# Attention with routed experts: gate probabilities made per batch and stored with the rows, one VectorE operation per expert tile, slot 30's row stores on SyncE's queue

## The chip, the cores and the metric

The kernel runs on one core of one Trainium2 chip. The metric is the device time of one execution in microseconds; lower is better. The core has five engines with instruction queues of their own: TensorE (PE in the profile, with its weight loads as PEld), VectorE (DVE), ScalarE (ACT), GpSimd (POOL) and SyncE (SP). Each works through its queue in order. Transfers are issued from SP's queue and from POOL's queue and are carried out by the same 16 DMA engines.

## The reference

Eight batches, eight heads, 576 positions, 64 columns a head. Causal attention in blocks of 64; its output, put side by side over the heads, is the input x (4608 rows of 512) of a layer of eight experts.

```
scores = scale * (q @ k^T), masked by blocks of 64;  attn = softmax(scores);  x = attn @ v
logits = x @ w_gate                     # 8 per row
local_gate = sigmoid(x @ w_local)
for s in rows of a batch:
    e = argmax(logits[s]) if s == 0 or local_gate[s] < 0.5 else the expert of row s-1
    p = softmax(logits[s])
    out[s] = p[e] * (relu(x[s] @ w1[e]) @ w2[e])
```

So each row goes through one expert, and its result is scaled by the probability of that expert.

## The kernel before

**Attention.** One pair of heads is a slot; slot i holds pair i of 32, four slots a batch, some 7.5 us each. In a slot PE computes scores (L957), ACT their Exp (L967), PE the product with v (L978, L987), DVE adds the partial sums (L999, L1001), and PE turns k and q of the next pair by transposes (L668, kq). POOL brings the k and q of the pair after that into order (L860), from loads that SP issues (L847). Work of the batch before is laid into the slots: `half_batch` multiplies x by the gate weights on PE (L681, trg), `logits_of` makes the logits in the tile `L` (PE trl, DVE L770 to L779), and `rows_of_batch` turns x into rows: PE transposes (trx), DVE multiplies by the softmax factor (L799) and writes 512 bf16 numbers of a row tile, and POOL copies the 8 logits of each row into the tail behind them (L794, L798). A row tile of 128 rows, x and logits, goes to the array `x_rows` in HBM by `store` and `release` (L653). Stores are held back until the end of a slot and then released on POOL's queue; the last ones, from the end of slot 31 on, on SP's queue. Row tiles are made in tiles `xg` or, for the late ones, in two buffers `x`, which a new row tile can only take when the old one's store has landed.

**Routing.** The generators `tokens`, `slots_first` and `slots_second` find the expert of each row and put rows of one expert together in tiles of 128 (index tables idx0 and idx1, one for batches 0 to 4, one for the rest). Their steps are laid between other work by the class `Steps`, by weights in the code; the order on each engine is therefore fixed when the program is built. The last group runs beside the first expert tiles (`late`), together with the row tiles of the last batch (`rows`, `rows_out`), and DVE does most of it.

**Expert tiles.** 38 tiles are computed; 15 come from the first table. For a tile POOL gathers 128 rows with their tails (L626), SP transposes x (a DMA transpose, L1357; the first four are issued in slot 30, L1246, behind the loads of that slot), DVE copies the expert's first weight (L1329; L1057 for the first two tiles), PE makes the first product (L1072, `first_mm`), ACT applies Relu (L1075), PE makes the second product (L1275, `second_mm`), ACT scales by the factor (L1283) and POOL scatters the rows to the output (L1286). The factor is the probability of the chosen expert, made from the 8 logits in the tail: `exps_of` takes their maximum on DVE (L1340) and Exp with its sum on ACT (L1341), `factor_of` picks the expert's value (L1347), takes the reciprocal of the sum (L1349) and multiplies (L1350). The gathers of the second table wait until routing's last group and the last batch's rows are done (`gathers`).

The 1 MB weight loads (L107, L111) run from POOL's queue, one every other slot; the last, of w2 of expert 7, is issued in slot 30.

Of the kernel before, what the change touches and what calls it, by code (L numbers as in the profile page):

```python
# [62 lines left out]
def kernel(  # L63
# [11 lines left out]
    nc = tc.nc  # L75
# [121 lines left out]
    lim = rt_c.tile([P, E], F32, tag="lim", name="lim")  # L197
    less_e = rt_c.tile([P, E], F32, tag="less_e", name="less_e")
# [118 lines left out]
    def tokens(c0, c1, T, A):  # L317
# [5 lines left out]
        lg = L[:, cs, :E]  # L323
        mx = T([P, n], "mx")
        nc.vector.reduce_max(mx, lg, axis=AX)
# [316 lines left out]
    held = []  # L642
# [89 lines left out]

    def rows_out(b, t):
# [21 lines left out]
    def logits_of(b):  # L755
# [8 lines left out]
        def out():  # L764
# [14 lines left out]
            nc.vector.reduce_sum(Lb[:ST, 4], tmp[:ST, 0].rearrange("q h e -> q e h"), axis=AX)  # L779
        return out  # L780

    def rows_of_batch(b, ts):
# [6 lines left out]
        def out():  # L789
# [3 lines left out]
            if kept:  # L793
                nc.gpsimd.tensor_copy(xg[:n, t0:t1, XH:], L[:n, NC * b + t0:NC * b + t1, :E])  # L794
            for j, t in enumerate(ts):
                x = xs[j]
                if not kept:
                    nc.gpsimd.tensor_copy(x[:n, XH:], L[:n, NC * b + t, :E])  # L798
# [11 lines left out]
    with tc.tile_pool(name="atn_const", bufs=1) as cst, \  # L810
# [340 lines left out]
        def behind(i):  # L1151
# [24 lines left out]
        for i in range(NPAIR):  # L1176
# [61 lines left out]
            if i < NPAIR - 1:  # L1238
                release(queue=nc.gpsimd)
# [27 lines left out]
    with tc.tile_pool(name="ffn_s", bufs=2, reuse_waits="tile") as f_p, \  # L1267
# [26 lines left out]
        def late():  # L1294
# [6 lines left out]
            yield "V", 0.4  # L1301
# [36 lines left out]
        def exps_of(x, f):  # L1338

            nc.vector.reduce_max(f[:, 16:17], x[:, XH:], axis=AX, negate=True)  # L1340
            nc.scalar.activation(f[:, :8], x[:, XH:], func=AF.Exp, bias=f[:, 16:17], scale=1.0,  # L1341
                                 accum_out=f[:, 17:18])
            return f

        def factor_of(ph, j, f):

            nc.vector.scalar_tensor_tensor(f[:, 8:16], less_e, ids[ph][:, j:j + 1], f[:, :8],  # L1347
                                           op0=ALU.is_equal, op1=ALU.mult, accum_out=f[:, 18:19])
            nc.vector.reciprocal(f[:, 17:18], f[:, 17:18])  # L1349
            nc.vector.tensor_mul(f[:, 19:20], f[:, 18:19], f[:, 17:18])  # L1350
            return f[:, 19:20]
# [129 lines left out]
```

## Time and profile before

| | |
|---|---|
| time, three runs | 416.65, 416.87, 421.27 us; median 416.87 |
| the profiled execution's own time | 415.86 us |
| its span | 414.1 us |
| PE busy | 395.3 us (95%) |
| DVE busy | 257.2 us (62%) |
| ACT busy | 234.2 us (57%) |
| POOL busy | 194.4 us (47%) |

A matmul's end is modelled in the records, so PE's busy time tells where PE had nothing to do rather than how fast it worked. Attention takes the span to about 253 us, the expert tiles the rest. In the rows of the order of time the first number is the start, the second the time from the first to the last end of the merged instructions; in square brackets stands the idle time before and what ended it. SPq and POOLq are the engines' sequencers, where transfers are issued.

### The profile page before, as it was taken

To read this page: it belongs to the slowest core of one execution; us is meant where nothing else is said; L and a number is where in the kernel's file an instruction comes from. 1 tells how busy PE (TensorE), PEld (TensorE's weight loads), DVE (VectorE), ACT (ScalarE), POOL (GpSimd) and SP (SyncE) were. 2 spreads that over 40 slices of the span, in tenths; PEclk is the share of its full clock that TensorE was granted. 3 is DMA by queue.
4 is the path that set the end of the run, shared out by engine and by line. 5 is a ranking of instruction groups with operands and counts; after the bars stand their busy time and mean duration, and the time that the engine had idled before them with its cause. 6 is when DMAs were issued, how large, how long until landed. Compare 5 with 4: busy or idle time off the path is not lost. (4 is left out here: it accounts for less than half of the span.)

```text
span 414.1 us, 14752 instructions
## 1 busy us (share of the span) xinstructions
PE 395.3 (95%) x5827; PEld 285.7 (69%) x5827; DVE 257.2 (62%) x652; ACT 234.2 (57%) x463; POOL 194.4 (47%) x263
## 2 busy tenths in 40 slices
PE   8999999999999999999998996999999999999985
PEld 7677776876866876766876674666676677767653
DVE  3443847557577877679899563888894454444430
ACT  4666665764764765754764564343454565555543
POOL 1346256146145155136244340655658556777703
PEclk9999999999999999999999999899999999999989
DMA  6479998998998989997989789344535644654522
GB/s 184 118 175 242 208 195 231 211 189 211 220 183 212 212 161 251 202 203 193 212 171 263 145 171 159 102 126 111 156 113 146 142 122 137 150 151 129 131 71 77
DMA packets 106677, 70.25 MB, mean 170 GB/s; under 512 B 72703, under 2 KB 98111, under 8 KB 106608
## 3 DMA queue, kind: packets, MB, share of 16 engines
q0 software_dynamic: 18880, 35.08, 39.8%
q1 hardware_dynamic: 87728, 34.21, 33.6%
q8 instruction: 48, 0.79, 0.8%
q14 instruction: 21, 0.17, 0.1%
HBM read 67.02 MB, written 14.83 MB: 198 GB/s over the span
## 5 line engine op out<-in xcount | busy, mean ns | idle before, releaser
L999 DVE TENSOR_TENSOR S<-S,Pc 128x896 f32<-128x896 f32 (+2 forms) x96 | 87.0, 906 | 19.9 <-PE o L978 15.3
L957 PE MATMUL sc<-qkT 64*64 64x224 f32 (+6 forms) x1536 | 90.9, 364 | 0.0
L860 POOL COPY w_bf<-w_bf 128x512 f32<-128x512 f32 x61 | 52.0, 870 | 64.5 <-DMA w_bf<-in_k_dram 49.7
L1072 PEld LDWEIGHTS <-w1c 128*128 128x128 bf16 x1152 | 67.9, 98 | 14.4 <-issue 6.9
L1329 DVE COPY w1c<-w_bf 128x4096 bf16 x36 | 44.9, 1248 | 48.4 <-PE ps_y L1275 25.1
L1275 PE MATMUL ps_y<-w_bf,hT 128*128 x304 | 73.2, 384 | 0.3 <-issue 0.2
L1072 PE MATMUL ps_h<-xT,w1c 128*128 128x128 bf16 x1088 | 68.5, 220 | 4.8 <-ACTq L1441 2.0
L957 PEld LDWEIGHTS sc<-qkT 64*64 64x64 f32 x1536 | 70.2, 133 | 2.0 <-issue 0.5
L967 ACT ACTIVATE Pc<-sc 128x448 f32<-128x448 f32 (+1 forms) x96 | 68.3, 718 | 0.0
L1286 POOL DMA_INDIRECT out_dram<-y,idx x38 | 47.2, 1242 | 40.8 <-ACT y L1283 22.4
L626 POOL DMA_INDIRECT xg<-x_rows,idx x38 | 48.8, 1285 | 26.8 <-ACT hT L1075 11.6
L1075 ACT ACTIVATE hT<-ps_h 128x512 bf16<-128x512 f32 x76 | 42.8, 587 | 29.0 <-PE ps_y L1275 14.8
L978 PE MATMUL o<-Pc,v 128*64 128x320 f32 (+2 forms) x512 | 57.3, 366 | 0.0
L978 PEld LDWEIGHTS o<-Pc,v 128*64 128x64 f32 x512 | 34.7, 137 | 23.9
L1275 PEld LDWEIGHTS <-hT 128*128 128x128 bf16 x304 | 28.4, 99 | 29.4 <-issue 3.2
L967 ACT ACTIVATE S<-sc 128x576 f32<-128x576 f32 x64 | 42.0, 656 | 11.4 <-PE sc L957 11.4
L991 ACT COPY oT<-o 128x576 f32<-128x576 f32 x32 | 20.5, 641 | 34.7 <-PE o L987 34.3
L978 PE MATMUL o<-S,v 128*64 128x192 f32 (+1 forms) x256 | 34.7, 392 | 1.7 <-ACT qkT L905 1.7
L1283 ACT ACTIVATE y<-ps_y,f 128x512 f32<-128x512 f32 (+1 forms) x38 | 25.8, 680 | 12.8 <-PE ps_y L1275 9.3
L799 DVE TENSOR_TENSOR xg<-trx,rs 128x512 bf16<-128x512 f32 (+1 forms) x31 | 20.2, 684 | 20.5 <-PE trx L668 20.4
L690 ACT COPY LT<-trg 128x320 f32<-128x320 f32 x15 | 6.4, 425 | 44.2 <-PE trg L681 40.4
L926 ACT COPY qkT<-kq 128x1024 f32<-128x1024 f32 x30 | 30.9, 1031 | 0.3 <-PE kq L668 0.3
(268 smaller groups left out, 474.1 us busy)
## 6 DMA issues: line engine op xcount, KB each, us to landing
w_bf<-in_moe_w_dram POOLq DMA_DIRECT2D x16, 1024.0 KB
w_bf<-in_k_dram SPq DMA_DIRECT2D x32, 256.0 KB
w_bf<-in_q_dram SPq DMA_DIRECT2D x32, 256.0 KB
v<-in_v_dram SPq DMA_DIRECT2D x64, 128.0 KB
x_rows<-xg POOLq DMA_DIRECT2D x24, 132.0 KB
qkl<-in_k_dram SPq DMA_DIRECT2D x32, 32.0 KB
qkl<-in_q_dram SPq DMA_DIRECT2D x32, 32.0 KB
vl<-in_v_dram SPq DMA_DIRECT2D x32, 32.0 KB
```

Of the source, the lines that this page charges most:

```text
L626: st = nc.gpsimd.indirect_dma_start(out=x, out_offset=None, in_=x_dram[:rows], in_offset=bass.IndirectOffsetOnAxis(ap=row_of(ph, j), axis= ...
L860: copies[j](m, raws[i][1 + j].rearrange("p h j d -> p j h d"))
L926: nc.scalar.copy(to.rearrange("p a (r s) -> p r a s", r=2), ps.rearrange("p r (a s) -> p r a s", a=2))
L957: nc.tensor.matmul(to[:, col + skip:col + n], lhsT=t[r, 0, k0:k0 + ST], rhs=t[r, 1, q0 + skip:q0 + n], start=True, stop=True)
L967: nc.scalar.activation(exps_at(i, c, q0, n, rows), ps[rows, :, col:col + n], func=AF.Exp, scale=scale_attn)
L978: nc.tensor.matmul(po[64 * h:64 * h + 64, VO + q0:VO + q0 + n], lhsT=vs[i][c][:, h, :], rhs=exps_at(i, c, q0, n, slice(0, P))[:, h, :], st ...
L999: nc.vector.tensor_add(Ss[i][:, :, P * c:], Ss[i][:, :, P * c:], Pc[i % 2][:, :, POS[c]:POS[c] + n])
L1072: nc.tensor.matmul(ps[:, fo, :], lhsT=w[:, ko * F + f0:ko * F + f0 + P], rhs=xT[:, ko, :], start=(ko == 0), stop=(ko == KO1 - 1))
L1075: relu[0] = nc.scalar.activation(hT[:, half * (FO // 2):(half + 1) * (FO // 2), :], ps, func=AF.Relu)
L1275: nc.tensor.matmul(ps, lhsT=hT[:, fo, :], rhs=w2_bf[:, bass.ds(ev + fo * Dm, Dm)], start=(fo == 0), stop=(fo == FO - 1))
L1286: st = nc.gpsimd.indirect_dma_start(out=out_flat, out_offset=bass.IndirectOffsetOnAxis(ap=row_of(ph, j), axis=0), in_=y, in_offset=None, b ...
L1329: ended["w"] = nc.vector.tensor_copy(w, w1_bf[:, bass.ds(ev[i], WE)])
```

## The change

Once a batch, right behind its logits, `probs_of` takes the maximum of the 8 logits of each row and subtracts it in place (DVE), and makes the Exp of all 128x40 differences (ACT). `sums_of_probs` makes the sums and their reciprocals (DVE); within attention it runs at the end of the next slot's additions, from the list `pending_sums`. Where the logits were copied into the rows' tails, `probs_into` now multiplies Exp by reciprocal into them, on POOL for batches 0 to 6 and on DVE for the last. `tokens` no longer takes the maximum itself, since the logits are already less their maximum. An expert tile's factor is then one DVE operation, which picks the expert's value from the tail and sums over the eight; `exps_of` is gone. It is made one step later than `exps_of` was, from a row tile that is one step older. Beside this, the row stores at the end of slot 30 are released on SP's queue instead of POOL's.

```diff
@@ tokens
-        lg = L[:, cs, :E]
-        mx = T([P, n], "mx")
-        nc.vector.reduce_max(mx, lg, axis=AX)
-        dl = T([P, n, E], "wide1")
-        nc.vector.tensor_sub(dl, lg, be(mx, n))
-        yield "V", 0.4 * k
         fe = T([P, n, E], "wide2")
-        nc.vector.scalar_tensor_tensor(fe, dl, 0.0, bt(w8, n), op0=ALU.is_ge, op1=ALU.mult)
+        nc.vector.scalar_tensor_tensor(fe, L[:, cs, :E], 0.0, bt(w8, n), op0=ALU.is_ge, op1=ALU.mult)
@@ new functions
+    def probs_of(b):
+        lg = L[:, NC * b:NC * b + NC, :E]
+        nc.vector.reduce_max(one_by, lg, axis=AX)
+        nc.vector.tensor_sub(lg, lg, be(one_by, NC))
+        nc.scalar.activation(probs, lg, func=AF.Exp)
+        return sums_of_probs
+
+    def sums_of_probs():
+        nc.vector.reduce_sum(one_by, probs, axis=AX)
+        nc.vector.reciprocal(one_by, one_by)
+
+    def probs_into(engine, x, t0, t1):
+        n, m = x.shape[0], t1 - t0
+        engine.tensor_tensor(x, probs[:n, t0:t1], one_by[:n, t0:t1, None].to_broadcast([n, m, E]),
+                             op=ALU.mult)
@@ rows_out (and alike in rows_of_batch, on nc.gpsimd)
-            nc.vector.tensor_copy(x[:n, XH:], L[:n, NC * b + t, :E])
+            probs_into(nc.vector, x[:n, None, XH:], t, t + 1)
@@ logits_of, at its end
+            pending_sums.append(probs_of(b))
@@ behind (a slot's work for the slot before)
             if not swap:
                 add_chunks(i - 1)
+            while pending_sums:
+                pending_sums.pop()()
@@ end of a slot
             if i < NPAIR - 1:
-                release(queue=nc.gpsimd)
+                release(queue=nc.gpsimd if i < NPAIR - 2 else nc.sync)
@@ late (last batch)
-            yield "V", 0.4
+            sums = probs_of(b)
+            yield "V", 0.6
+            sums()
             yield from tokens(*GROUPS[2], TS, A2)
@@ expert tiles
-        def exps_of(x, f):
-            nc.vector.reduce_max(f[:, 16:17], x[:, XH:], axis=AX, negate=True)
-            nc.scalar.activation(f[:, :8], x[:, XH:], func=AF.Exp, bias=f[:, 16:17], scale=1.0,
-                                 accum_out=f[:, 17:18])
-            return f
-        def factor_of(ph, j, f):
-            nc.vector.scalar_tensor_tensor(f[:, 8:16], less_e, ids[ph][:, j:j + 1], f[:, :8],
-                                           op0=ALU.is_equal, op1=ALU.mult, accum_out=f[:, 18:19])
-            nc.vector.reciprocal(f[:, 17:18], f[:, 17:18])
-            nc.vector.tensor_mul(f[:, 19:20], f[:, 18:19], f[:, 17:18])
-            return f[:, 19:20]
+        def factor_of(ph, j, x, f):
+            nc.vector.scalar_tensor_tensor(f[:, :E], less_e, ids[ph][:, j:j + 1], x[:, XH:],
+                                           op0=ALU.is_equal, op1=ALU.mult, accum_out=f[:, E:])
+            return f[:, E:]
@@ loop over the tiles
             if i:
-                factor = factor_of(*tiles[i - 1], fs)
-            fs = exps_of(xgs[i % NX], f_p.tile([P, 20], F32, tag="f", name="f", bufs=3))
+                factor = factor_of(*tiles[i - 1], xgs[(i - 1) % NX],
+                                   f_p.tile([P, E + 1], F32, tag="f", name="f"))
```

The order on SP's queue at the end of slot 30 and beyond, before (L653 are row stores, L1246 the transposes of the first four expert tiles, L1357 those of later tiles):

```order
L1246 DMA_TRANSPOSE S<-xg 128x4x128 x4
L653 DMA x_rows<-x 128x264 x2
L1357 DMA_TRANSPOSE xT<-xg 128x4x128 x2
L653 DMA x_rows<-x 128x264
L1357 DMA_TRANSPOSE xT<-xg 128x4x128 x2
L653 DMA x_rows<-x 128x264
L1357 DMA_TRANSPOSE xT<-xg 128x4x128 x2
```

The same place after the change (L649, L1262 and L1366 are the same lines of code):

```order
L649 DMA x_rows<-x 128x264 x2
L649 DMA x_rows<-xg 64x264
L1262 DMA_TRANSPOSE S<-xg 128x4x128 x4
L649 DMA x_rows<-x 128x264 x2
L1366 DMA_TRANSPOSE xT<-xg 128x4x128 x2
L649 DMA x_rows<-x 128x264
L1366 DMA_TRANSPOSE xT<-xg 128x4x128 x2
```

Slot 30's three stores have come in front of the first four transposes.

DVE's queue at the end of routing, before, beside expert step 11 (L1329 is the weight copy, L1347 to L1340 the factor's operations, L742 and L743 the last row tile, L429 the second index table):

```order
L742 COPY x<-L 64x8
L743 TENSOR_TENSOR x<-trx,rs 64x512
L1082 TENSOR_LOAD et_93
L1329 ISA
L1329 COPY w1c<-w_bf 128x4096
L1347 SCALAR_TENSOR_TENSOR f<-less_e,ids_89,f 128x8
L1349 RECIPROCAL f<-f 128x1
L1350 TENSOR_TENSOR f<-f 128x1
L1340 TENSOR_REDUCE f<-xg 128x1
L578 TENSOR_TENSOR S<-S,rti 128x56
L603 TENSOR_TENSOR S<-S 128x28
L604 TENSOR_SCALAR S<-S 128x28
```

After the change (L1347 is the weight copy, L1358 the factor, L425 the index table, L743 and L756 the row tile):

```order
L599 TENSOR_TENSOR S<-S 128x28
L600 TENSOR_SCALAR S<-S 128x28
L425 SCALAR_TENSOR_TENSOR idx_94<-S 128x28
L1096 TENSOR_LOAD et_95
L1347 ISA
L1347 COPY w1c<-w_bf 128x4096
L1358 SCALAR_TENSOR_TENSOR f<-less_e,ids_91,xg 128x8
L743 TENSOR_TENSOR x<-probs,one_by 64x8
L756 TENSOR_TENSOR x<-trx,rs 64x512
```

The factor is one operation; the index table is made a step earlier, and the last row tile (64 rows) has moved behind it, a step later than it was.

POOL's queue where the gathers of the second table begin, before (L626 gathers, L1286 scatters of results):

```order
L626 DMA xg<-x_rows,idx_91 128x264
L1286 DMA out_dram<-y,idx_91 4608x512 x2
L626 DMA xg<-x_rows,idx_92 128x264 x2
L1286 DMA out_dram<-y,idx_91 4608x512
L626 DMA xg<-x_rows,idx_92 128x264
```

After the change (L622 and L1302):

```order
L622 DMA xg<-x_rows,idx_93 128x264
L1302 DMA out_dram<-y,idx_93 4608x512 x3
L622 DMA xg<-x_rows,idx_94 128x264 x3
L1302 DMA out_dram<-y,idx_93 4608x512
L622 DMA xg<-x_rows,idx_94 128x264
```

The first gather of the second table comes one expert step later, and three are issued together.

More of the change, by code (lines that the diff above doesn't have):

```diff
@@ L197 @@
     lim = rt_c.tile([P, E], F32, tag="lim", name="lim")
+    probs = rt_c.tile([P, NC, E], F32, tag="probs", name="probs")
+    one_by = rt_c.tile([P, NC], F32, tag="one_by", name="one_by")
     less_e = rt_c.tile([P, E], F32, tag="less_e", name="less_e")
@@ L640 @@
     pending = []
-    held = []
+    held, pending_sums = [], []
     holding = [False]
@@ L797, in out @@
                 if not kept:
[L798 removed]
+                    probs_into(nc.gpsimd, x[:n, None, XH:], t, t + 1)
                 nc.vector.tensor_mul(
@@ L1384, in more_tiles @@
             x, y = (old[:, o:o + 2 * n].bitcast(F32) for n in (XW, Dm))
-            f = old[:, o + 2 * Dm:o + 2 * Dm + 40].bitcast(F32)
+            f = old[:, o + 2 * Dm:o + 2 * Dm + 2 * E + 2].bitcast(F32)
             for ph, j in more:
@@ L1449 @@
                 reason="begun before")
-        second_mm(*tiles[i], prev, ev.pop(i), factor_of(*tiles[i], fs), both=True)
+        second_mm(*tiles[i], prev, ev.pop(i), factor_of(*tiles[i], xgs[i % NX],
+                                                               f_p.tile([P, E + 1], F32, tag="f", name="f")), both=True)
 _INS = ['q', 'k', 'v', 'moe_w_gate', 'moe_w_local', 'moe_w1', 'moe_w2']
```

4 lines of the change are left out of this document (2 added, 2 removed).

## The prediction

> **What bounds the kernel now.** I read the stretches of the span first, to see where TensorE (PE) is not busy; then the order of time around the one large hole; then the waits. Columns of the stretch rows: length, then busy PE, PEld, DVE, ACT, POOL, then the granted clock, the DMA share, GB/s.
>
> ```profile
> 250.00:260.00 10.00, 6.25 (x86) 4.42 (x83) 4.05 (x5) 3.02 (x5) 1.47 (x4) 0.99 0.86 156
> 280.00:300.00 20.00, 18.68 (x205) 13.19 (x202) 17.82 (x60) 8.23 (x21) 12.14 (x9) 1.00 0.51 132
> 330.00:360.00 30.00, 30.00 (x344) 21.93 (x342) 14.85 (x54) 17.99 (x44) 19.52 (x16) 1.00 0.49 130
> ```
>
> At 330 to 360 PE has no idle time: what DVE or ACT save there is hidden behind PE. At 280 to 300 DVE is 89% busy and PE loses 1.3 us. At 250 to 260, where attention hands over to the expert tiles, PE loses 3.75 us. The order of time there:
>
> ```profile
> 243.70 1.29 DVE L799 TENSOR_TENSOR x<-trx,rs 128x512 bf16<-128x512 f32 x2 [3.29 <-PE trx L668]
> 244.90 0.67 DVE L799 TENSOR_TENSOR xg<-trx,rs 64x512 bf16<-64x512 f32 x1
> 244.80 0.93 POOL L111 DMA_DIRECT2D w_bf<-in_moe_w_dram  x1 [1.78 <-DVE x L799]
> 245.72 1.13 POOL L653 DMA_DIRECT2D x_rows<-x  x2
> 256.60 1.29 DVE L799 TENSOR_TENSOR x<-trx,rs 128x512 bf16<-128x512 f32 x2 [5.95 <-DMA x_rows<-x]
> 257.80 1.22 DVE L1057 COPY qkT<-w_bf 128x4096 bf16 x1
> 252.94 1.96 PE L1072 MATMUL ps_h<-S,Pc 128*128 128x128 bf16 x32
> 258.03 0.75 PE L681 MATMUL trg<-oT,wg 128*32 128x320 f32 x8 [3.13 <-DVE x L799]
> 259.40 3.23 PE L1072 MATMUL ps_h<-S,qkT 128*128 128x128 bf16 x32 [0.62 <-DVE qkT L1057]
> 262.56 1.58 PE L681 MATMUL trg<-S,sel 128*32 128x320 f32 x16
> 242.68 6.16 SPq L1246 DMA_TRANSPOSE S<-xg  x4
> ```
>
> Slot 30's row stores leave POOL at 245.72, right behind a 1 MB weight load, and free their two x buffers only about 256.5, 10.8 us later. DVE's row products of slot 31 need those buffers, PE's gate sums need the PSUM bank that these products empty, so PE stands still for 3.1 us and then 0.6 us more for the weight copy queued behind them on DVE. The hole also costs clock:
>
> ```profile
> 252.98:256.40 3.42, 1.92 (x36) 1.75 (x32) 0.00 (x0) 1.83 (x3) 0.00 (x0) 1.00 1.08 222
> 256.40:259.81 3.41, 1.15 (x16) 0.66 (x17) 3.21 (x4) 0.42 (x1) 1.28 (x4) 1.00 0.25 84
> 259.81:263.22 3.41, 3.41 (x36) 2.88 (x37) 2.51 (x7) 0.39 (x2) 2.42 (x3) 0.50 0.20 53
> 392.93:396.34 3.41, 1.40 (x25) 1.41 (x25) 1.68 (x6) 1.57 (x4) 1.16 (x2) 1.00 0.64 155
> 396.34:399.75 3.41, 3.41 (x18) 1.79 (x16) 1.68 (x6) 1.19 (x2) 0.00 (x0) 0.50 0.22 82
> ```
>
> Stretches of 3.41 us with 1.15 and 1.40 us of PE work are each followed by one at clock 0.50; the one with 1.92 us is not. The price here: 3.23 us for 32 products that took 1.96 us just before, so 1.3 us, and 0.3 us for the 0.66 us of gate sums that lie inside that stretch: 1.6 us.
>
> **The change part by part.**
>
> 1. *Slot 30's stores on SP's queue.* They are issued when DVE's products are done (the first ends near 244.4), about 244.5 and 245.1, ahead of the weight load's bytes and no longer behind them. But SP issues in order, and the four transposes of the first expert tiles, which in the old kernel began at 242.68, now stand behind the third store, which needs the DVE product that ends at 245.57. They begin about 246.05, 3.4 us later, when the weight load is running. When does the first land, which PE needs at 252.94? Rows for a transfer of SP's queue with and without a weight load beside it:
>
> ```profile
> 231.21 0.82 POOL L107 DMA_DIRECT2D w_bf<-in_moe_w_dram  x1
> 232.69 0.37 SPq L847 DMA_DIRECT2D w_bf<-in_k_dram  x1
> 241.39 1.24 POOL L860 COPY w_bf<-w_bf 128x512 f32<-128x512 f32 x2 [8.19 <-DMA w_bf<-in_k_dram]
> 265.25 1.19 SPq L1357 DMA_TRANSPOSE xT<-xg  x1
> 267.50:268.50 1.00, 1.00 (x19) 0.88 (x17) 0.93 (x4) 0.11 (x1) 0.70 (x2) 1.00 0.00 0
> 257.00:258.00 1.00, 0.00 (x0) 0.00 (x0) 1.00 (x3) 0.00 (x0) 0.20 (x1) 1.00 0.00 0
> ```
>
> A transpose issued at 265.25 with little beside it is through by 267.5, since the DMA share is then 0: 2.3 us. A load of k issued 1.5 us after a weight load reached its reader 8.7 us later. And the DMA engines carry nothing from 257 on: everything queued here, whatever its order, is moved by then. So the first transpose lands between 248.4 and 257.0. The nearer rows are those under a weight load, 8.7 us (k) and 10.8 us (the stores), and I take 9.2: 255.3. PE then waits 2.4 us at 252.94, a new wait in the place of the old. From there: 1.96 us of products, 0.75 us of gate sums, 0.1 us of gaps, so the second tile's products start at 258.15 instead of 259.40 (DVE's row products and its weight copy are then long done: even if the stores take 8.7 us, they land at 253.8, and 1.29 + 1.22 us later it is 256.3). Gain 1.25 us, between -0.4 (257.0) and 3.7 us (in time). A hole of 2.4 us lies inside one 3.41 us stretch often but not always; I credit a quarter of the 1.6 us of clock: 0.4. In time, all 1.6 are saved: 5.2 us together.
>
> [...]
>
> 2. *One DVE operation per expert tile.* ACT's Exp and DVE's reciprocal, product and maximum go, for each of 38 tiles:
>
> ```profile
> L1341 ACT ACTIVATE f<-xg,f 128x8 f32<-128x8 f32 x38 | 11.3, 298 | 33.7 <-issue 19.2 <-DVE f L1340 9.0 <-ACT y L1283 3.3
> L1341 ACT ACTIVATION_READ_ACCUMULATOR f<-xg,f 128x1 f32 x38 | 7.1, 187 | 0.0
> L1350 DVE TENSOR_TENSOR f<-f 128x1 f32<-128x1 f32 x38 | 6.0, 159 | 1.3
> L1349 DVE RECIPROCAL f<-f 128x1 f32<-128x1 f32 x38 | 5.9, 156 | 0.0
> L1340 DVE TENSOR_REDUCE f<-xg 128x1 f32<-128x8 f32 x38 | 5.8, 153 | 0.0
> PE ps_h L1072 <- DVE f L1349: 0.9, 3, 0.5
> PE rtb L352 <- DVE S L349: 0.5, 1, 0.5
> ```
>
> That is 0.49 us of ACT and 0.47 us of DVE a tile, 18.4 and 17.7 us in all, nearly all of it beside a PE that is never idle. It counts only while routing's last group shares DVE (264 to 310, 11 tiles, 5 us less on DVE). There PE waited 0.9 us in a queue of DVE work and 0.5 us within routing's own chain, and at the rate of 280 to 300 it loses 3.0 us in all. The 0.9 go; of the rest I count 0.1: 1.0 us, between 0 and 3.0.
>
> 3. *Probabilities per batch.* Added, in each of 8 batches: a maximum, a subtraction, a sum and a reciprocal on DVE, one Exp on ACT, and products on POOL or DVE where copies stood. Not in the trace; by the nearest rows (156 to 278 ns) the four are 0.7 us of DVE a batch, while two 128x120 operations of routing go in three places (0.55 us each):
>
> ```profile
> L325 DVE TENSOR_REDUCE w_bf<-L 128x15 f32<-128x120 f32 x1 | 0.3, 278 | 0.0
> 140.41 0.27 DVE L779 TENSOR_REDUCE L<-ltmp 64x9 f32<-64x72 f32 x1
> 141.41 0.64 ACT L991 COPY oT<-o 128x576 f32<-128x576 f32 x1 [1.64 <-PE o L987]
> ```
>
> The place to look at is ACT: its queue is in order, and the Exp stands ahead of the copy of o (L991). DVE's logits end at 140.68; maximum and subtraction bring that to about 141.05, the Exp (0.3 us) to 141.4, just when the copy starts anyway after 1.64 us of idling. Cost 0, cover nearly used up; without it at most 0.35 us in each of 7 batches, 2.5 us. On POOL the product now waits for the sums behind the next pair's additions and delays the copies of k and q by up to 4 us, which PE needs a slot (7 to 8 us) later: 0. The bound for the product itself is its copy, 0.2 us, up to a few tenths more; POOL idles for us around it.
>
> 4. *Routing's last steps move.* The last row tile (64 rows) is now transposed after the second product of step 11, and the gathers of the second group wait for its store:
>
> ```profile
> 305.37 0.60 PE L696 MATMUL trx<-id_f,oT 128*64 128x128 f32 x4
> 307.88 1.89 PE L1275 MATMUL ps_y<-w_bf,hT 128*128 x8
> 309.82 2.00 POOL L626 DMA_INDIRECT xg<-x_rows,idx  x1 [0.83 <-DVE idx L429]
> 313.70 1.19 SPq L1357 DMA_TRANSPOSE xT<-xg  x1
> 320.72 0.22 PE L1072 MATMUL ps_h<-xT,w1c 128*128 128x128 bf16 x1
> ```
>
> That moves 305.37 to 309.6; 1.6 us to the store (as before, 307.0) and 2.1 us for it give a first gather at 313.3, 3.5 late. It needs 3.9 us to its transpose and that 2.3 us: 319.5, against tile 15's products at 320.7. Cost 0 with 1.2 us of cover left, up to 2.3 us (3.5 less 1.2) if there is none; I take 0.15, since the cover is thin.
>
> Sum: 1.25 + 0.4 + 1.0 - 0.15 = 2.5 us, on the profiled execution's 415.86 us (span 414.1): 413.4. That execution lies 1.0 us under the median of the three runs, 416.87, which would become 414.4; I state 414.0, between them.
>
> **The rivals.**
>
> *The hole closes.* For it: the transposes go first on an almost empty queue, and unloaded they need 2.3 us; even 6.9 us would do. Against it: the k row, 8.7 us. Then 5.2 + 1.0 - 0.15 = 6.05 off 415.86, and the same half microsecond up: 410.4. [...]
>
> *The hole only changes its name.* The transposes land with everything else, at 257.0: part 1 gives -0.4, the clock drops as before, and part 2's gain is the 0 of its lower end. 416.9.
>
> *ACT's queue, slower.* In each of seven batches the Exp waits for DVE's subtraction while the copy of o, and all of the next slot's Exps, wait behind it. It decides where DVE's logits start over 0.3 us later against PE than in the row above. Price 0.35 us for the Exp and up to as much for a late subtraction, 7 times: 4.9; with the hole unchanged about 420.5. Against it: at 140.4 the two just fit, and PE has three score banks to run ahead.
>
> That DVE work does not shrink is excluded by the order of its instructions; that the stores stay behind the weights, too.
>
> **How the numbers follow.** A new, smaller wait: 0.45. The hole closes: 0.25. It only changes its name: 0.18. ACT's queue or a later gather, slower: 0.12. The likeliest gives 414.0, its own range 412 to 416. Leaving out no more than 2 in 10, with two thirds of part 2's upper 3.0 us on top of a closed hole and part of the slower case, the range is 408.8 to 418.5. Two per cent, about what a measurement of this kernel tells from no change, is 8.3 us: faster than 408.5 needs the hole closed and nearly part 2's upper end, 0.06; slower than 425.2 needs more than ACT's whole price, 0.03; within, 0.91.
>
> **What would show it.** Right: POOL's and DVE's waits for x_rows<-x before slot 31's rows gone; PE idle about 2 to 2.5 us right before the first tile's ps_h<-S,Pc, put down to the transposes; the gate sums straight behind that tile; no wait of PE for DVE f; the attention stretches unchanged to 0.3 us. Wrong: the first tile's products still at 252.9 and clock 1.00 after them (the hole closed), a stretch of attention longer by over 1 us (ACT's queue), or PE idle before tile 15.

## The result, and the profile after

The changed kernel takes 419.51 us (median of 20 runs, 416.74 to 425.21), against 415.46 us for the kernel before in 20 runs of the same comparison (412.90 to 421.27). The ratio is 1.008, 95% interval 1.0056 to 1.0104: about 3.3 us slower, where 2.5 us faster was forecast, and above the end of the range. The ratio is of the fast runs of each kernel, without executions over 1.5% above its fastest (here one of each kernel); the two medians are over all runs and 4.1 us apart. The profiled execution of after took 417.05 us (span 415.3 us, mean granted clock 0.996); that of before 415.86 us (414.1 us, 0.991). The two spans differ by only 1.2 us, with more clock lost in before's profile. If a span is longer by the share of clock it lost (an estimate, not shown), that is 0.9% of 414.1 or 3.7 us in before, 0.4% of 415.3 or 1.7 us in after. With these 2.0 us the pair comes to 3.2 us, which agrees with the ratio.

Where the time goes is read from one instruction that comes once a slot, ACT's copy of o (L991 before, L1005 after). First before, slots 4, 17, 18, 27 and 31 in the order of time, then after:

```profile
42.81 0.65 ACT L991 COPY oT<-o 128x576 f32<-128x576 f32 x1
...
141.41 0.64 ACT L991 COPY oT<-o 128x576 f32<-128x576 f32 x1 [1.64 <-PE o L987]
149.98 0.65 ACT L991 COPY oT<-o 128x576 f32<-128x576 f32 x1
...
219.39 0.64 ACT L991 COPY oT<-o 128x576 f32<-128x576 f32 x1 [2.10 <-PE o L987]
...
253.10 0.64 ACT L991 COPY oT<-o 128x576 f32<-128x576 f32 x1 [2.34 <-PE o L987]
```

```profile
43.89 0.65 ACT L1005 COPY oT<-o 128x576 f32<-128x576 f32 x1
...
142.49 0.62 ACT L1005 COPY oT<-o 128x576 f32<-128x576 f32 x1
151.61 0.64 ACT L1005 COPY oT<-o 128x576 f32<-128x576 f32 x1
...
221.04 0.64 ACT L1005 COPY oT<-o 128x576 f32<-128x576 f32 x1 [2.10 <-PE o L1001]
...
257.08 0.64 ACT L1005 COPY oT<-o 128x576 f32<-128x576 f32 x1 [2.34 <-PE o L1001]
```

After is 1.08 us late at slots 4 and 17, 1.63 at slot 18, 1.65 at slot 27 and 3.98 at slot 31. The first 1.08 us is lost between slots 3 and 4 and also in profiles of kernels with the old attention; the first of the added operations runs at 49.85 us, behind slot 4. So it is no effect of the change. The other 2.9 us are lost between slots 4 and 31, in attention. The stretch behind it, before and then after (columns as in the prediction):

```profile
250.00:264.00 14.00, 10.25 (x124) 7.28 (x120) 7.15 (x11) 3.41 (x7) 4.49 (x6) 0.88 0.69 132
```

```profile
250.00:264.00 14.00, 10.51 (x177) 8.04 (x174) 8.44 (x13) 5.46 (x9) 3.19 (x5) 1.00 1.02 151
```

At the hand-over the clock is now 1.00 (0.88 before). PE's waits after:

```profile
PE ps_h L1086 <- DMA S<-xg: 3.5, 1, 3.5
...
PE ps_h L1086 <- DVE f L1358: 2.4, 2, 1.4
...
PE rti L502 <- DVE ltmp_f L492: 0.8, 1, 0.8
...
PE trg L677 <- POOL S L1020: 0.4, 1, 0.4
```

The wait for DVE's row products (3.1 us) is gone; a wait of 3.5 us for the transposes stands in its place. The first second product of tile 0 starts at 266.14 instead of 264.08, so 1.9 of the 4.0 us are given back here, and at tile 12 after is 1.1 us late: another 1.0 given back. The second products of tiles 0 and 12, before and then after:

```profile
264.08 1.90 PE L1275 MATMUL ps_y<-w_bf,hT 128*128 x8
...
314.90 1.89 PE L1275 MATMUL ps_y<-w_bf,hT 128*128 x8
```

```profile
266.14 1.90 PE L1291 MATMUL ps_y<-w_bf,hT 128*128 x7
...
315.98 1.89 PE L1291 MATMUL ps_y<-w_bf,hT 128*128 x8
```

The wait behind DVE's factor has grown from 0.9 to 2.4 us. POOL, in the order of time, before (L794 copy of logits, L107 weight load, L653 row stores, L626 gather) and after (L743 product, L107, L649, L622):

```profile
202.45 0.20 POOL L794 COPY xg<-L 128x16 f32<-128x16 f32 x1 [2.99 <-DVE rs L776]
...
209.03 0.80 POOL L107 DMA_DIRECT2D w_bf<-in_moe_w_dram  x1 [0.28 <-issue]
209.83 1.09 POOL L653 DMA_DIRECT2D x_rows<-xg  x2
...
228.82 1.09 POOL L626 DMA_INDIRECT xg<-x_rows,idx  x1 [4.16 <-DMA x_rows<-xg]
...
231.21 0.82 POOL L107 DMA_DIRECT2D w_bf<-in_moe_w_dram  x1
```

```profile
210.66 0.21 POOL L743 TENSOR_TENSOR xg<-probs,one_by 128x16 f32<-128x16 f32 x1 [9.43 <-DVE one_by L739]
210.82 1.16 POOL L874 COPY w_bf<-w_bf 128x512 f32<-128x512 f32 x2
212.04 0.20 POOL L1020 MEMSET S<- 64x128 f32 x1
212.19 0.82 POOL L107 DMA_DIRECT2D w_bf<-in_moe_w_dram  x1
213.00 1.10 POOL L649 DMA_DIRECT2D x_rows<-xg  x2
...
232.37 1.00 POOL L622 DMA_INDIRECT xg<-x_rows,idx  x1 [5.44 <-DMA x_rows<-xg]
...
234.68 0.82 POOL L107 DMA_DIRECT2D w_bf<-in_moe_w_dram  x1
```

The product costs 0.21 us, the same as the copy. But it waits 9.43 us for `one_by`, and behind it in POOL's queue stand not only the copies of k and q but the memset of S, a weight load, the row stores, and later the gathers, which wait for those stores to land. The weight load that left at 209.03 leaves at 212.19; the one that left at 231.21 leaves at 234.68, so 3.2 and 3.5 us later, where ACT's copy of slot 27 is 1.65 us late. (In a_dve below, whose product is not on POOL, the first of the two leaves at 211.93, 2.9 us later than in before, where slot 26 is 2.4 us late: only 0.5 us more than the slots.) At slot 18 the queue is seen to reach PE in the same slot:

```profile
147.69 0.20 DVE L738 TENSOR_REDUCE one_by<-probs 128x5 f32<-128x40 f32 x1
147.92 0.19 DVE L739 RECIPROCAL one_by<-one_by 128x5 f32<-128x5 f32 x1
148.33 0.21 POOL L743 TENSOR_TENSOR xg<-probs,one_by 128x16 f32<-128x16 f32 x1 [9.94 <-DMA w_bf<-in_q_dram]
148.50 1.16 POOL L874 COPY w_bf<-w_bf 128x512 f32<-128x512 f32 x2
149.37 1.87 PE L677 MATMUL trg<-S,sel 128*32 128x320 f32 x16
149.72 0.20 POOL L1020 MEMSET S<- 64x128 f32 x1
149.97 0.41 PEld L677 LDWEIGHTS trg<-S,sel 128*32 128x32 f32 x10 [0.48 <-POOL S L1020]
```

The profile puts the wait down to a DMA into `w_bf`, which the product does not read; what it reads is `one_by`, ready when the reciprocal ends at 148.11. The copies and the memset come behind it, PE's gate sums need the memset, and the 16 sums take 1.87 us. In before they took 1.26:

```profile
148.33 1.26 PE L681 MATMUL trg<-S,sel 128*32 128x320 f32 x16
```

That is the 0.55 us between slots 17 and 18.

### The profile page after: what moved, and what is told of

Its sections match the earlier page's. It is cut to its first block, busy times and chain, and to the rows that moved or that the text cites. A ratio compares the mean times of both kernels' runs of the same rounds, so it can differ in the third digit from the quotient of the medians.

```text
span 415.3 us, 14631 instructions
## 1 busy us (share of the span) xinstructions
PE 393.4 (95%) x5805; PEld 285.1 (69%) x5827; DVE 244.9 (59%) x564; ACT 226.4 (55%) x395; POOL 179.1 (43%) x260
## 4 chain that ended last, share of the span: by engine, by line
PE 71%; DMA 12%; DVE 7%; issue 5%; POOL 2%; ACT 2%; SPq 1%; POOLq 0%; DVEq 0%; ACTq 0%
PE o L992 16%; PE sc L971 15%; PE ps_h L1086 12%; PE ps_y L1291 10%; PE trg L677 6%; DMA out_dram<-y,idx 4%; PE kq L664 4%; DMA S<-xg 2%; DMA w_bf<-in_q_dram 2%; DMA qkl<-in_k_dram 2%; PE trx L664 2%; PE o L1001 2%; PE o L664 1%; DVE S L1013 1%; PE sc L966 1%
## 5 line engine op out<-in xcount | busy, mean ns | idle before, releaser
L1013 DVE TENSOR_TENSOR S<-S,Pc 128x896 f32<-128x896 f32 (+2 forms) x96 | 83.4, 869 | 20.3 <-PE o L992 15.9
L1347 DVE COPY w1c<-w_bf 128x4096 bf16 x36 | 44.9, 1248 | 62.2 <-PE ps_h L1086 43.2
L1089 ACT ACTIVATE hT<-ps_h 128x512 bf16<-128x512 f32 x76 | 44.2, 598 | 54.9 <-PE ps_h L1086 36.5
L1291 PE MATMUL ps_y<-w_bf,hT 128*128 x282 | 67.7, 379 | 1.4 <-issue 0.2
L622 POOL DMA_INDIRECT xg<-x_rows,idx x38 | 47.4, 1248 | 48.0 <-ACT hT L1089 15.7
L874 POOL COPY w_bf<-w_bf 128x512 f32<-128x512 f32 x61 | 42.6, 717 | 55.7 <-DMA w_bf<-in_k_dram 38.4
L1302 POOL DMA_INDIRECT out_dram<-y,idx x38 | 44.1, 1161 | 31.2 <-ACT y L1299 14.6
L1005 ACT COPY oT<-o 128x576 f32<-128x576 f32 x32 | 20.4, 638 | 23.1 <-PE o L1001 23.0
```

The costliest lines, as they stand in the source:

```text
L622: st = nc.gpsimd.indirect_dma_start(out=x, out_offset=None, in_=x_dram[:rows], in_offset=bass.IndirectOffsetOnAxis(ap=row_of(ph, j), axis= ...
L874: copies[j](m, raws[i][1 + j].rearrange("p h j d -> p j h d"))
L1013: nc.vector.tensor_add(Ss[i][:, :, P * c:], Ss[i][:, :, P * c:], Pc[i % 2][:, :, POS[c]:POS[c] + n])
L1089: relu[0] = nc.scalar.activation(hT[:, half * (FO // 2):(half + 1) * (FO // 2), :], ps, func=AF.Relu)
L1291: nc.tensor.matmul(ps, lhsT=hT[:, fo, :], rhs=w2_bf[:, bass.ds(ev + fo * Dm, Dm)], start=(fo == 0), stop=(fo == FO - 1))
L1302: st = nc.gpsimd.indirect_dma_start(out=out_flat, out_offset=bass.IndirectOffsetOnAxis(ap=row_of(ph, j), axis=0), in_=y, in_offset=None, b ...
```

## The experiments

Two theories were set against each other at first. **W**: the loss is POOL's wait, with all that stands behind it in the queue. **C**: it comes from DVE's longer routing steps. Later ones split W. Each ratio is to the kernel before, measured beside it on the same chip; each group of runs had another chip, so a difference of two ratios is often one between chips. The number of runs is 12 where no other is given.

**b_rel** is before with part 1 alone, **b_ffn** before with part 2 alone (its factor picks a logit instead of a probability).

```diff
# b_rel
-                release(queue=nc.gpsimd)
+                release(queue=nc.gpsimd if i < NPAIR - 2 else nc.sync)
# b_ffn
-        exps_of, factor_of(ph, j, f)      (five operations)
+        factor_of(ph, j, x, f)            (one operation)
```

> The kernel before with only slot 30's three row stores moved to SP's queue. Theory R (the release is the loss: four transposes stand behind the stores, the first expert tile starts 7 us late and the clock falls more often): slower than before by 2 to 4 us. Theory A (the loss sits in attention, with the per-batch probabilities; the release trades one 3 us hole for another): within 1 us of before, or 1 to 2 us faster as my prediction's part 1 had it, with PE's wait for S<-xg near 2.4 us.

> The kernel before with only the expert tiles' factor as one VectorE operation (the rows still carry raw logits, so Exp, sum and reciprocal are left out altogether; attention, routing and the stores' queue are those of before). Prediction's part 2: 1.0 us faster (0 to 3.0), because VectorE's queue is shorter while routing runs. Theory F (the tail of a gathered row is now read a step later, its buffer comes free later, the next gather and transpose start later): slower than before by 1 us or more, PE idle before some tile between 318 and 335 us.

b_rel: 415.55 us, ratio 0.9991 (0.9957 to 1.0025). b_ffn: 415.27 us, 0.9998 (0.9962 to 1.0034). Neither alone moves the time by what can be told; the 1.0 us expected of part 2 does not show. In b_rel's waits the hole is there as in after:

```profile
PE ps_h L1072 <- DMA S<-xg: 3.4, 1, 3.4
```

**a_norel** is after with slot 30's stores back on POOL, **a_copy** is after once more.

```diff
# a_norel
-                release(queue=nc.gpsimd if i < NPAIR - 2 else nc.sync)
+                release(queue=nc.gpsimd)
```

> The changed kernel with slot 30's stores back on POOL's queue. Theory R: the loss of 3.3 us is gone, 414 to 416. Theory A: the loss stays, 418 to 420, the attention stretch is as long as in the changed kernel (copy of o of slot 31 near 257 instead of 253 us), and VectorE's wait for the x buffers before slot 31's rows is back (3 us of PE).

> The changed kernel itself once more, for a second profile on the chip of the other three. What repeats is the change's doing: theory A expects attention 3 to 4 us longer again, with the losses before slots 4, 18, 29 and 30; if these stalls come from transfers that merely happened to meet, they move to other slots or go, and the loss has to show elsewhere. Time 418 to 420.5 either way.

a_norel: 421.68 us (6 runs), 1.0143 (1.0096 to 1.0190). a_copy: 418.42 us, 1.0063 (1.0031 to 1.0096). The loss repeats, and it is not part 1: without part 1 it is larger, by 0.8%, and larger than the 418 to 420 us expected. So on top of part 3 the move of the stores wins something, though b_rel shows no gain from it; why is not shown. a_copy's order of time shows PE at slot 29 standing for POOL's copies of k and q:

```profile
237.35 1.01 PE L664 MATMUL kq<-id_f,w_bf 64*128 64x64 f32 x16 [1.22 <-POOL w_bf L874]
```

**a_dve**, **a_defer**, **b_wait**: the product on VectorE; the product still on POOL but moved just ahead of the row stores; and before with one DVE operation (logits times 1.0) behind the additions, for which POOL's copy then waits.

```diff
# a_dve (likewise for single row tiles)
-                probs_into(nc.gpsimd, xg[:n, t0:t1, XH:], t0, t1)
+                probs_into(nc.vector, xg[:n, t0:t1, XH:], t0, t1)
# a_defer (the list is emptied at the start of release)
+                products.append(lambda: probs_into(nc.gpsimd, xg[:n, t0:t1, XH:], t0, t1))
# b_wait (the list is emptied behind the additions)
+            pending_sums.append(lambda: nc.vector.tensor_single_scalar(lg, lg, 1.0, op=ALU.mult))
```

> The changed kernel with the per-batch product done by VectorE, right behind the reciprocal it needs, instead of POOL: the same arithmetic, VectorE 0.2 to 0.4 us longer a batch, and POOL waits for nothing new. Theory W (the loss is POOL's queue: its product waits 9 to 10 us for the sums, and the copies of k and q, the memset of S, the weight loads, the row stores and the gathers behind it start 2 to 4 us late): the loss of attention goes (copy of o of slot 31 at 253 us again, no step at slots 18 and 29) and with the other two parts the kernel comes to 411 to 414. Rival D (VectorE's four added operations or ACT's Exp are the loss): unchanged or slower, 418 to 420.

> The changed kernel with POOL's product moved in POOL's own order to just ahead of the row stores that need it: behind the copies of k and q, the memset of S and the weight load, which no longer wait. Theory W: most of the loss goes, 412 to 415; the stores alone may still be late. Rival D: 418 to 420.

> The kernel before with only the wait: one VectorE operation (the logits times one, in place, 0.2 us) stands where the changed kernel has its sums, behind the pair's additions, and POOL's copy of the logits waits for it. No Exp, no sums, no product, the old queue and the old expert tiles. Theory W: 2.5 to 4 us slower than before, 418 to 419.5, with steps of 0.5 us before slot 18 and 2 to 3 us before slot 29. Rival D: within 1 us of before.

a_dve: 416.85 us, 1.0008 (0.9975 to 1.0042). a_defer: 418.16 us, 1.0030 (0.9996 to 1.0063). b_wait: 417.18 us, 1.0027 (0.9990 to 1.0065). All lie between before and after. None meets what W asked (411 to 414, 412 to 415, and 418 to 419.5 us with a step at slot 18 that b_wait does not have), and a_dve is not the 418 to 420 of its rival either. Against after's 0.80% and a_copy's 0.63%, a_dve brings back 0.55 to 0.72% (less, some 0.3 to 0.45%, by the two other kernels below that also have the product on VectorE); putting a wait into before costs 0.27%, which the interval does not tell from nothing.

**b_relffn** is before with parts 1 and 2 (factor as in b_ffn); **a_chain** is a_dve with the last group's DVE steps cut smaller, which theory C wants.

```diff
# a_chain, in late
+            yield "V", 0.4
             sums = probs_of(b)
-            yield "V", 0.6
+            yield "V", 0.4
             sums()
+            yield "V", 0.6
```

> The kernel before with slot 30's stores on SP's queue and the one-operation factor together, and no per-batch probabilities (rows carry raw logits, so the softmax is left out). It is the changed kernel without its attention part, the ceiling of what parts 1 and 2 can give. If their gains add and stay (2 us less from slot 31's copy of o to the first second product, 2.5 us less to the twelfth tile, as the two profiles had them): 411 to 412.5. If the clock takes them back (more half-clock stretches after the holes that stay): 414 to 416, as each of the two alone.

> The changed kernel with the product on VectorE, as in the run before that, and routing's last chain cut into pieces as small as in the old kernel: maximum, subtraction and Exp in a piece of their own, the sums in another, instead of joined to their neighbours. Theory C (the changed kernel's 1.4 us wait of PE for f near the sixth tile is a piece of routing that grew too long for one step of PE): that wait goes, 0.8 to 1.2 us less up to the twelfth tile than with the product on VectorE alone, 415 to 416. Rival: VectorE is simply fuller and the wait only moves: no change, 416.5 to 417.

b_relffn: 415.47 us, 0.9955 (0.9920 to 0.9991): the two parts together are worth 0.45%, or 1.9 us (0.1% by the two alone; the intervals allow both). a_chain: 417.62 us, 1.0035 (1.0003 to 1.0066). Its PE waits for the factor no more, but:

```profile
PE ps_h L1086 <- DVE x L743: 1.2, 1, 1.2
PE rti L502 <- DVE ltmp_f L492: 1.2, 1, 1.2
```

The wait went in part to the next row product on DVE. In its profile a_chain still gives back 2.3 us from tile 0 to tile 12, a_dve 1.1, as theory C had it; but the time of the whole kernel is no better. Theory C names a real wait, and removing it wins no time that can be told.

**a_shift** leaves out Exp, sums and product in batches 0 to 6: there the tails hold logits less their maximum, which POOL copies. **a_dve_oldend** is a_dve with the end of routing as before (logits in the last batch's tails). **b_nomax** is before with part 1 and without the maximum in a tile's softmax, with the same result for these logits.

```diff
# a_shift (and the copies of before for the products)
-            pending_sums.append(probs_of(b))
+            nc.vector.reduce_max(one_by, lg, axis=AX)
+            nc.vector.tensor_sub(lg, lg, be(one_by, NC))
# b_nomax
-            nc.vector.reduce_max(f[:, 16:17], x[:, XH:], axis=AX, negate=True)
-            nc.scalar.activation(f[:, :8], x[:, XH:], func=AF.Exp, bias=f[:, 16:17], scale=1.0,
+            nc.scalar.activation(f[:, :8], x[:, XH:], func=AF.Exp, scale=1.0,
```

> The changed kernel in which batches 0 to 6 keep only the maximum and the subtraction (the routing needs them): no Exp, no sums, no product, and POOL copies the shifted logits as the old kernel did, so those rows carry no probabilities. VectorE keeps 0.4 us of the added 0.9 to 1.2 us a batch, POOL waits for nothing behind the pair's additions. Theory W: about as the changed kernel with the product on VectorE or faster, 0.0 to 0.4% faster than before. If VectorE's added operations in attention are what that kernel still loses, it gains another 1 to 2 us on it, 0.2 to 0.5% faster than before; if the loss that is left sits in routing's end, it stays at no change.

> The changed kernel with the product on VectorE in batches 0 to 6, and routing's end as in the old kernel: no maximum, Exp and sums for the last batch in the chain, its rows carry raw logits, and the selection makes its own maximum again. If routing's end costs 1 to 2 us (PE's 1.4 us wait for f and the later gathers of the second group): 0.3 to 0.5% faster than before. If attention holds the rest: no change against before.

> The kernel before with slot 30's stores on SP's queue and the maximum left out of each tile's softmax (Exp of the logits as they are; the same probabilities as long as no logit overflows): 0.15 us less on VectorE a tile and one wait less of ACT. A version, not a test of the attention part. If VectorE's time in the first eleven tiles is worth what the one-operation factor showed (2.5 us for 0.47 us a tile), a third of it: 0.8 us, with the stores 0.1 to 0.4% faster than before; if the clock takes it back, no change.

a_shift: 420.02 us, 1.0093 (1.0056 to 1.0129): as slow as the change, without any wait of POOL for sums. So W alone does not carry the loss; the maximum and the subtraction ahead of the additions must cost, too, by DVE's time or because POOL's copy now waits for the subtraction. a_dve_oldend: 417.82 us, 1.0036 (0.9997 to 1.0074), no better than a_dve, so the new end of routing shows no cost. b_nomax: 414.96 us, 0.9950 (0.9905 to 0.9994), faster than both kernels.

Then a ladder on b_relffn, with routing as in before (its own maximum and subtraction included, which the change takes out): **c_shift** adds maximum and subtraction, **c_nopool** also Exp and sums, **c_all** also POOL's product, and **c_wait** has the wait of b_wait alone. **c_dveonly** writes maximum and subtraction into a tile that nobody reads, and POOL copies the raw logits.

```diff
# c_shift                                  # c_dveonly: probs for the second lg
+            nc.vector.reduce_max(one_by, lg, axis=AX)
+            nc.vector.tensor_sub(lg, lg, be(one_by, NC))
# c_nopool, c_all
+            pending_sums.append(probs_of(b))
# c_all
-                nc.gpsimd.tensor_copy(xg[:n, t0:t1, XH:], L[:n, NC * b + t0:NC * b + t1, :E])
+                probs_into(nc.gpsimd, xg[:n, t0:t1, XH:], t0, t1)
```

> A ladder of four, all with the stores on SP's queue, the one-operation factor and routing's end as in the old kernel; the rows' tails carry other numbers than the softmax asks for. Without any attention part this kernel was 0.45% faster than before. Rung 1: batches 0 to 6 get only the maximum and the subtraction on VectorE ahead of the pair's additions; POOL copies the shifted logits. If 0.4 us of VectorE in that place is the loss: 0.4% slower than before or more. If POOL's wait for the sums is the loss: still 0.2 to 0.5% faster.

> Rung 2: as rung 1, and ACT's Exp and VectorE's sum and reciprocal behind the additions are there too, but POOL still copies the shifted logits and so waits only for the subtraction. If the four VectorE operations and the Exp cost by themselves: slower than rung 1 by 0.2% or more. If POOL's wait is the loss: as rung 1.

> Rung 3: as rung 2, with POOL's product in place of the copy, so that it waits for the sums: the whole attention part of the change, without routing's end. If POOL's wait is the loss: 0.5 to 0.9% slower than rung 2 and about as slow as the changed kernel, 0.4 to 0.8% slower than before. If it is not: as rung 2.

> The wait alone on the same footing: no maximum, no subtraction, no Exp, no sums; one VectorE operation of 0.2 us (the logits times one) behind the pair's additions, and POOL's copy waits for it. If POOL's wait is the loss: 0.5 to 0.9% slower than the kernel without an attention part, so 0 to 0.5% slower than before. If not: 0.4% faster than before.

> Rung 1 of the ladder without its wait: VectorE makes the maximum and the subtraction at the same place, ahead of the pair's additions, but into a tile that nobody reads, so that POOL copies the raw logits as soon as they are there, as in the old kernel. Stores, factor and routing's end as on the other rungs. If VectorE's 0.4 us ahead of the additions is what rung 1 lost: 0.1 to 0.5% slower than before, as rung 1. If POOL's later copy is: 0.2 to 0.6% faster than before, as the kernel without an attention part.

c_shift: 417.52 us, 1.0030 (0.9998 to 1.0063). c_nopool: 416.57 us, 1.0025 (0.9994 to 1.0056). c_all: 418.06 us, 1.0062 (1.0028 to 1.0096). c_wait: 414.44 us, 0.9976 (0.9943 to 1.0010), 0.2% above b_relffn. c_dveonly: 410.95 us, 0.9983 (0.9960 to 1.0007; that chip ran the kernel before in 411.82 us). From b_relffn's 0.9955, part 3 in attention costs 1.07%, about 4.4 us, with an interval of some 0.6 to 1.6%. Maximum and subtraction make 0.75% of it when POOL's copy waits for the subtraction (c_shift), 0.28% when it does not (c_dveonly); Exp and sums make nothing that can be told, POOL's product 0.37% (c_all less c_nopool). Each of these differences is good to some 0.45% either way, so the whole and c_shift's 0.75% are clear of zero, and the rest of the split is only indicated. c_dveonly and c_wait fell between what their two theories asked: neither DVE's time alone nor POOL's wait alone is shown to cost.

**a_late** moves maximum and subtraction behind the additions and everything else to DVE and ACT.

> The changed kernel, whole and exact, with its per-batch work moved in the order: maximum and subtraction behind the pair's additions, Exp behind ACT's copy of k and q at the slot's end, then VectorE's row products, the sums and, on VectorE too, the product. POOL has none of it. If the place of maximum and subtraction is the loss, and POOL's waits the rest: 0.1 to 0.5% faster than before. If VectorE's added time costs wherever it stands: as the changed kernel with the product on VectorE, 0 to 0.4% slower than before.

485.77 us (6), 1.1795 (1.1749 to 1.1841). In its order routing reads the logits before the maximum is taken off (DVE reads them at 111.87 us, L326 of that kernel; the subtraction of the last of these batches, L733, comes only at 116.06), so its tables were others, and the time answers nothing that was asked.

**Where each loses.** The lateness of ACT's copy of o against before, in us, gained between two slots of the profiled executions:

| kernel | slot 7 to 12 | 17 to 18 | 27 to 31 | 4 to 31 |
|---|---|---|---|---|
| after | 0.0 | 0.55 | 2.33 | 2.90 |
| a_copy | 0.0 | 0.55 | 3.00 | 3.56 |
| a_norel | 0.0 | 0.55 | 1.98 | 2.68 |
| c_all | 0.0 | 0.55 | 1.46 | 2.17 |
| a_dve | 0.0 | 0.0 | 1.91 | 2.08 |
| a_dve_oldend | 0.0 | 0.0 | 1.97 | 2.97 |
| a_chain | 0.0 | 0.0 | 1.33 | 1.39 |
| a_defer | 0.0 | -0.06 | 1.98 | 1.87 |
| a_shift | 2.86 | 0.0 | 0.54 | 3.56 |
| c_shift | 2.44 | 0.0 | 1.82 | 4.49 |
| c_nopool | 2.60 | 0.0 | 1.13 | 3.71 |
| c_dveonly | 2.26 | 0.0 | 2.26 | 5.16 |
| c_wait, b_wait | 0.0 | 0.0 | 0.72, 1.00 | 0.72, 0.99 |
| b_rel, b_ffn, b_relffn, b_nomax | 0.0 | 0.0 | -0.33, 0.74, 0.14, -0.19 | -0.35, 0.68, 0.13, -0.26 |

All twelve kernels of the table with DVE's maximum and subtraction in attention lose 1.4 to 5.2 us there, the six without at most 1.0. The 0.55 us at slot 18 stands in exactly the four kernels in which POOL's product, waiting for the sums, stands ahead of the copies and the memset. In the four that have maximum and subtraction and a copy of logits on POOL, the loss at slots 8 and 12 comes instead. So DVE's time alone is not it: c_all and c_nopool have the same DVE work, and only c_nopool loses 2.6 us there.

The loss from slot 27 to 31 goes with one instruction of POOL, the gather that waits for a row store to land. In after it starts at 232.37 instead of 228.82, 3.55 us late where slot 27 is 1.65 us late: 1.9 us more. Behind it in POOL's queue stand a weight load and the copies of k and q. Over the eighteen kernels of the table this excess and the loss from slot 27 to 31 rise together (correlation 0.94), with POOL's product and without it. That is an association; no run moved the gather alone, and PE's waits do not name it.

All these are single executions, and some lie far from the median of their kernel: c_dveonly's took 415.14 us against 410.95, a_dve's 420.47 against 416.85, c_shift's 420.47 against 417.52. What they lose is more than the kernels usually lose, so the table says where and not how much.

## Why the prediction was wrong

**The step that failed is part 3**: "On POOL the product now waits for the sums behind the next pair's additions and delays the copies of k and q by up to 4 us, which PE needs a slot (7 to 8 us) later: 0." The wait was foreseen, but only one of the things queued behind it was priced. The memset of S is needed in the same slot (0.55 us at slot 18). The weight load and the row stores leave 3.2 us late, twice what the slots around them are late. And the copies of k and q are not always a slot ahead: a_copy's PE stood 1.22 us for them. The bound of 2.5 us belonged to ACT's Exp, not to POOL. DVE's maximum and subtraction ahead of the additions got no price of their own. Measured, part 3 in attention costs 1.07% or about 4.4 us, where the prediction's sum had 0. With the 1.9 us that parts 1 and 2 win together this makes 2.5 us slower; the 0.8 us up to the measured 3.3 lie within the intervals.

**The rival on the slower side had the right sign and the wrong place.** It put the loss on ACT. After's Exp stands right before the copy of o and delays nothing that PE needs:

```profile
142.35 0.24 ACT L734 ACTIVATE probs<-L 128x40 f32<-128x40 f32 x1 [1.52 <-DVE w_bf L310]
142.49 0.62 ACT L1005 COPY oT<-o 128x576 f32<-128x576 f32 x1
```

The copy at slot 17 is as late as at slot 4, and c_nopool, which adds Exp and sums to c_shift, is not measurably slower.

**Part 1** went as forecast in kind: a new wait of PE, put down to the transposes, and the gate sums straight behind the tile. Its size was off:

```profile
250.12 7.97 SPq L1262 DMA_TRANSPOSE S<-xg  x4
260.48 1.95 PE L1086 MATMUL ps_h<-S,Pc 128*128 128x128 bf16 x32 [3.49 <-DMA S<-xg]
262.36 0.74 PE L677 MATMUL trg<-oT,wg 128*32 128x320 f32 x8
```

The product starts 10.4 us after the transposes begin, where 9.2 were taken; the hole is 3.5 us, not 2.4. In before it was 3.1 and 0.6, so the hole itself is hardly smaller. What after won is mostly clock (1.00 against 0.88 from 250 to 264 us), of which the prediction credited a quarter, and that did not repeat: in a_copy, the same kernel, the same 32 products behind the same hole took 3.17 us, not 1.95, at a clock of 0.85 and then 0.65 (259.81 to 263.22 and to 266.63).

```profile
261.74 3.17 PE L1086 MATMUL ps_h<-S,Pc 128*128 128x128 bf16 x32 [3.52 <-DMA S<-xg]
```

In before a transpose with little beside it was through in 2.3 us. In after it is 10.4 us from the first of the four issues to the product, and 4.6 us from the last, issued at 255.9. Which of the four ended PE's wait the trace does not say.

**Part 2** was right in after's profile by the sum (1.0 us from tile 0 to tile 12), but not by the step: PE's waits for f grew. In b_ffn the same stretch gives 2.5 us, in c_all, with the routing of before, 2.2, and in a_chain, with smaller steps, 2.3; so the last batch's longer DVE steps took the rest, as far as single profiles show. In the times, parts 1 and 2 together are worth 1.9 us; 2.65 were forecast.

**Part 4** was taken at 0.15 us, and the runs show no more. After's PE idles 1.98 us (1.06, 0.52 and 0.40) near tiles 13 and 14, where before's four idle times sum to 1.02. But kernels with the routing's end of before idle there as long, a_dve_oldend 1.93 and b_rel 1.76 us, and nowhere does the profile show what PE waits for. First after, then a_dve_oldend:

```profile
320.56 0.22 PE L1086 MATMUL ps_h<-xT,w1c 128*128 128x128 bf16 x1 [1.06 <-issue]
```

```profile
321.10 1.79 PE L1092 MATMUL ps_h<-xT,w1c 128*128 128x128 bf16 x26 [1.06 <-issue]
```

So this idle time is not put down to the later gathers, and in the times a_dve against a_dve_oldend shows no cost of the new end either.

**What stays open** is by what road DVE's maximum and subtraction cost up to 3 us. In c_nopool a late memset (0.32 us) and then a late load of v (1.16 us) show as waits of PE, and the DMA share is 0.48 for 4 us between stretches with 1.09 and 1.15 (the last row is before's, in the middle stretch, with 1.11):

```profile
64.00:72.00 8.00, 8.00 (x132) 5.70 (x132) 4.93 (x7) 4.70 (x8) 2.43 (x5) 1.00 1.09 282
72.00:76.00 4.00, 3.68 (x62) 2.09 (x58) 1.69 (x3) 1.04 (x3) 3.84 (x7) 1.00 0.48 89
76.00:84.00 8.00, 8.00 (x153) 6.35 (x144) 4.89 (x12) 6.28 (x12) 1.07 (x2) 1.00 1.15 218
...
72.00:76.00 4.00, 4.00 (x90) 3.08 (x82) 1.05 (x2) 2.83 (x6) 1.14 (x3) 1.00 1.11 166
```

```profile
73.34 1.27 PE L683 MATMUL trg<-S,sel 128*32 128x320 f32 x12 [0.32 <-POOL S L1026]
101.83 1.05 PE L998 MATMUL o<-S,v 128*64 128x192 f32 x7 [1.16 <-DMA v<-in_v_dram]
```

That a delay of a transfer in such a phase is not made good would fit these rows. It is argued from them; no run shows it, since none keeps the DVE work and takes the transfers away.

## What to carry to other kernels

When an operation on an engine's queue begins to wait, price every entry behind it, transfers and memsets too, by who needs each one first. That the engine is often idle was no cover here: POOL is busy for 43% of after's span, and the weight load behind the product that waited 9.43 us still left 3.2 us late. Nor should small work ahead of transfers be counted as free because its engine has idle time: here 0.4 us of it a batch on DVE (busy for 59% of after's span), with the wait that it brought, cost 0.75% in c_shift, by a road that stays open; the DMA share in attention was 0.93 (60 to 250 us in after). And a part of a change that wins (here 1 and 2, or the maximum left out) should be timed without the part it came with.

## What the runs showed of the hardware

- The clock did not follow PE's work in 3.41 us as simply as the prediction's rows suggest. In before a stretch with 1.15 us of work has one at clock 0.50 behind it; after's hole has a stretch with 0.59 us, and the next is at 1.00 (before's ends where the clock falls; after has no drop there to place one by). What sets the clock is not shown, so neither is the quarter of the 1.6 us that the prediction credited. Behind holes of 3.3 to 3.5 us the 32 products took 1.95 us in after and b_rel, 3.17 in a_copy and 3.31 in b_relffn.

```profile
256.40:259.81 3.41, 0.59 (x12) 0.21 (x8) 3.08 (x6) 0.64 (x1) 0.00 (x0) 1.00 1.08 157
259.81:263.22 3.41, 2.74 (x44) 2.15 (x45) 0.14 (x1) 0.60 (x1) 1.74 (x2) 1.00 0.74 183
```

- Over the 162 runs of the kernel before that stood beside the experiments, on six chips, 0.004 less of mean clock goes with 1.3 us more (correlation -0.48; -0.40 to -0.73 on the single chips). So a part of the spread between runs of one kernel goes with the clock; for the two profiles the estimate above puts it at 2.0 us.
- About 1 us is lost or not between slots 3 and 4, in kernels of both sorts: 0.0 in b_rel and 1.0 in b_relffn, whose attention is the same.
